# First tokens with tokens on partitions in a fused attention and feed-forward kernel; the low bits of the weights move from GpSimd to ScalarE

## The chip, the cores and the metric

The kernel runs on one core of a Trainium2 chip. The metric is device time in microseconds (us), from the launch of the program to its end; the time before is 574.05 us (median of 3 runs, 573.91 to 575.09). Engines are named as in the profile: PE is TensorE, DVE VectorE, ACT ScalarE, POOL GpSimd, SP SyncE, whose queue issues the DMAs.

## The reference

```
q, k, v: (4, 8, 576, 64)   M_prev: (4, 8, 64, 64)   z_prev: (4, 8, 64)   beta: (8,)
a     = softmax(q @ k.T / 8, causal);        local = a @ v
q_p   = elu(q) + 1
mem   = (q_p @ M_prev) / (q_p @ z_prev + 1e-6)
g     = sigmoid(beta)
attn  = g * mem + (1 - g) * local            # (4, 8, 576, 64)
x     = attn as 2304 tokens x 512 (head and feature together)
out   = relu(x @ w_in) ** 2 @ w_out          # w_in 512 x 2048, w_out 2048 x 512
```

Inputs and output are float32.

## The kernel before

**Products.** The feed-forward part runs in fp16 with each operand as a high and a low half: three matmuls stand for one product (hi·hi, hi·lo, lo·hi; L940 to L942 for `up`, the first layer, and L912 to L914 for `oacc`, the second).

**Weights.** They come as 32 pieces of 512 KB: eight groups of four, w_in and w_out in turn. The float32 bits of a piece arrive in a 64-bit number. `to_float` puts them together: ACT shifts the upper word (L194), the low three bits are made by POOL for two pieces of three (L191, 21 pieces) and by DVE for the third (L193, 11 pieces), and DVE joins both into `fc` (L196). `weight_scale` finds one scale for a group: 16 matmuls (`gr`, L222), a maximum over rows (L225), one over partitions (L203, L204), a power of two (L210, L213) and its reciprocal. `halves` then writes the high half (ACT, L240) and the low half (DVE, L241). The first 16 pieces use one set of buffers, the others a second one: loads from piece 16 on (L266, SP's queue) wait until buffers of the first set are free, and the float piece 28 takes the buffer of piece 20, so it waits for the halves of 20.

**Attention.** A unit is one batch, one pair of heads and some tiles of tokens; batches 0 and 1 run their tiles 1 and 2 for all four head pairs, then 3 and 4, batches 2 and 3 all four tiles at once. Scores are `sp` (L558), their maxima `mx` (L579), exponentials `e` (L599), the normed weights `a` (L637, L639), which go through a DMA transpose to `aT`; `acc` (L663) is weights times values, added into `feat` (L666). The memory part is `pe` (elu, L463 to L475), `pm` (L522) and `nm` (L527, L531).

**First tokens.** Tile 0 of every batch, 64 tokens x 4 batches, is computed on its own in `first_tokens`, in two groups g of two batches, so that the feed-forward part has a first block of 256 tokens (`moe(0)`) before any attention unit is done. Both heads of a pair stand on the partitions, a feature on each, tokens beside one another. For one group: scores, `phi` (elu features, then the norm `nr`, its reciprocal, 16 matmuls `rb` that spread it over partitions, and a product), `softmax`, and `outputs`: transposed weights `px`, the sum `xp` of memory and local part (features on partitions), its squares, their sums over features for each token by matmuls with ones (`nm`), a power of two and its reciprocal over 128 x 128 (`qn`, `sn`, L390), the product `xs` (L392), high half (L394) and low half (L395), which go straight into `xT`, the operand of `moe(0)`.

**Later blocks.** `moe(1)` to `moe(6)` take 256 tokens each from `feat`: squares (L689), scale, halves `hl` (L696, L697), a DMA transpose into `xT` (L698). The last two blocks are computed together in another way.

**Order.** `ORD` merges generators: the first attention unit with 17 steps of weights, then units 1 to 3 with the weights' steps up to 34 and `moe(0)`, then the other units one after the other. From these a tile scheduler writes each engine's order; each engine works through its list in that order. Up to unit 3 a unit's rows follow one another, from unit 4 (`FIRST`) on the next unit is begun ("whole": loads, scores and features ahead) before the rows of this one. Values of `gate` ("v", "s", "t") mark instructions of the first tokens behind which other work of the same engine is held.

Of the kernel before, what the change touches and what calls it, by code (L numbers as in the profile page):

```python
# [78 lines left out]
FIRST = 4  # L79
WE = 8  # L80
# [17 lines left out]
def fused_kernel(ctx: ExitStack, tc: tile.TileContext, t0_d, kk_d, qv_d, beta, w_in, w_out, out):  # L98
# [22 lines left out]
    onesb = cp.tile([P, P], BF16, name="onesb")  # L121
    nc.vector.memset(onesb, 1.0)
# [36 lines left out]

    gate = {}  # L160
# [143 lines left out]
    def first_tokens(tp, ahead):  # L304
# [4 lines left out]
        tr, sp, et, ft = ({} for _ in range(4))  # L309
# [27 lines left out]
        def phi(g):  # L337
            q, z = part(g, 0), tr[g][:, 2 * GD : TA]
            ft[g] = f = tp.tile([P, GN, D], F32, tag="f", name="f", bufs=2)
            t2 = tp.tile([P, GN], F32, tag="t2", name="t2", bufs=2)  # L340
# [4 lines left out]
            for i, hd in pairs():  # L345
                nc.tensor.matmul(nr[hd, i : i + 1], f[hd, i], z[hd, i : i + 1], start=True, stop=True)
            nc.vector.scalar_tensor_tensor(out=t2, in0=nr, scalar=1e-6, in1=gib, op0=ALU.add, op1=ALU.mult)
            nc.vector.reciprocal(t2, t2)
            rb = ps.tile([P, GN, D], F32, tag="av", name="rb", bufs=2)
            for i, hd in pairs():  # L350
                nc.tensor.matmul(
                    rb[hd, i], t2[hd, i : i + 1].to_broadcast([D, D]), ident[hd, hd], start=True, stop=True
                )
            nc.vector.tensor_tensor(out=f, in0=f, in1=rb, op=ALU.mult)

        def softmax(g):
# [10 lines left out]
            nc.vector.reciprocal(t1, t1)  # L367
            gate["v"] = nc.vector.tensor_tensor(out=e, in0=e, in1=t1[:, :, None].to_broadcast(bc), op=ALU.mult)

        def outputs(g):  # L370
# [5 lines left out]
            m, v = part(g, TA), part(g, TA + GD)  # L376
            xp = ps.tile([P, GN, D], F32, tag="av", name="xp", bufs=2)
            for i, hd in pairs():
                at_i = xp[hd, i % NP * GB + i // NP]
                nc.tensor.matmul(at_i, m[hd, i], ft[g][hd, i], start=True, stop=False)  # L380
                gate["t"] = nc.tensor.matmul(at_i, v[hd, i], ex[hd, i], start=False, stop=True)
            xb = xp.rearrange("p (i b) q -> p i (b q)", b=GB)
            sq = tp.tile([P, NK, P], BF16, tag="sq", name="sq", bufs=2)
            nc.scalar.activation(sq, xb, AF.Square)
            nm = ps.tile([P, P], F32, tag="acc", name="nm0", bufs=2)
            for k in range(NK):
                nc.tensor.matmul(nm, onesb, sq[:, k], start=k == 0, stop=k == NK - 1)
            q, s = (tp.tile([P, P], F32, tag=t, name=t, bufs=1) for t in ("qn", "sn"))
# [4 lines left out]
            hi, lo = (xT[:, g, k * NK : (k + 1) * NK] for k in range(2))
            gate["s2"] = nc.scalar.copy(hi, xs)  # L394
            gate["v2"] = nc.vector.tensor_tensor(out=lo, in0=xs, in1=hi, op=ALU.subtract)  # L395
            qc = ps.tile([P, 1], F32, tag="acc", name="qc", bufs=2)
            nc.tensor.matmul(qc, q.bitcast(BF16).rearrange("p (n t) -> p n t", t=2)[:, :, 1], identb[:, :1], start=True, stop=True)
            nc.scalar.activation(tok0[:, g : g + 1], qc, AF.Square, scale=WSC / HSC)
# [707 lines left out]
```

## Time and profile before

| | |
|---|---|
| time, median of 3 runs | 574.05 us (573.91 to 575.09) |
| the profiled execution: its own time | 575.25 us |
| its span, first to last instruction | 573.5 us |
| PE busy | 531.8 us (93%), clock 0.973 |
| DVE busy | 456.3 us (80%) |
| ACT busy | 398.1 us (69%) |
| POOL busy | 60.1 us (10%) |

Busy time is that of instructions that compute; PE's clock is the share of full speed that was granted. A row of the timeline gives start, duration, engine, line, output and inputs; what stands in brackets at its end is the engine's idle time before it and what ended it. Starts of neighbouring instructions are a little nearer than durations say, since they overlap at the ends. The profiled execution's 575.25 us is 1.75 us more than its span and 1.20 us above the median.

### The profile page before, as it was taken

How to read it: one execution, taken by the hardware profiler on the slowest of the kernel's cores; microseconds unless marked ns; L12 is line 12 of the kernel's file. 1: busy time of each engine (PE TensorE's matmuls, PEld its weight loads, DVE VectorE, ACT ScalarE, POOL GpSimd, SP SyncE). 2: the span in 40 equal slices, each digit the busy share in tenths (PEclk: the TensorE clock that was granted, in tenths of full speed). 3: DMA queues.
4: the chain of work that ended last, by engine and by line, in shares of the span. 5: the costliest groups of instructions: out<-in, count | busy, mean ns of one | idle time of the engine just before them, and what ended most of it. 6: DMA issues, size and time to landing. Idle time of an engine off the chain costs nothing.

```text
span 573.5 us, 12883 instructions
## 1 busy us (share of the span) xinstructions
PE 531.8 (93%) x4903; PEld 378.3 (66%) x4903; DVE 456.3 (80%) x1413; ACT 398.1 (69%) x853; POOL 60.1 (10%) x41
## 2 busy tenths in 40 slices
PE   6587997799989799999999999999899999999997
PEld 6375774576757577667767667767666756447766
DVE  6989789998888978999779878887685888544745
ACT  3566897776787797988868887887676644457352
POOL 3660584001010000000000000000000000000000
PEclk9957999699999999999999999999999999999999
DMA  8921796365657876987396476562656510100002
GB/s 311 405 98 38 259 353 167 82 141 122 136 138 150 150 164 147 164 175 197 95 151 121 119 153 114 81 117 69 112 105 74 98 20 2 38 0 1 2 1 73
DMA packets 131022, 70.87 MB, mean 124 GB/s; under 512 B 113296, under 2 KB 119440, under 8 KB 130960
## 3 DMA queue, kind: packets, MB, share of 16 engines
q1 hardware_dynamic: 130960, 70.05, 51.8%
q8 instruction: 38, 0.62, 0.4%
q14 instruction: 24, 0.20, 0.1%
HBM read 37.53 MB, written 4.72 MB: 74 GB/s over the span
## 4 chain that ended last, share of the span: by engine, by line
PE 32%; DVE 29%; ACT 12%; DMA 7%; issue 4%; SPq 0%; ACTq 0%; DVEq 0%
DVE a L639 6%; DVE e L579 6%; DMA aT<-a 4%; ACT e L599 4%; PE seven L815 4%; PE up L940 3%; PE up L941 3%; PE up L942 3%; PE oacc L913 3%; PE oacc L912 3%; PE oacc L914 3%; ACT a L637 3%; PE seven L788 2%; PE seven L786 2%; PE seven L787 2%
## 5 line engine op out<-in xcount | busy, mean ns | idle before, releaser
L940 PE MATMUL up<-xT,w 128*128 128x256 f16 x448 | 123.7, 277 | 3.2 <-DMA xT<-hl 2.6
L941 PE MATMUL up<-xT,w 128*128 128x256 f16 x448 | 123.7, 276 | 0.0
L942 PE MATMUL up<-xT,w 128*128 128x256 f16 x448 | 123.6, 276 | 0.0
L599 ACT ACTIVATE e<-e,mx 128x320 f32<-128x320 f32 (+3 forms) x128 | 77.5, 607 | 45.2 <-DVE feat L666 27.5
L912 PE MATMUL oacc<-w,gh 128*128 128x512 f16 x224 | 85.0, 379 | 2.3 <-ACT gh L949 2.3
L913 PE MATMUL oacc<-w,gh 128*128 128x512 f16 x224 | 84.9, 379 | 0.0
L914 PE MATMUL oacc<-w,gl 128*128 128x512 f16 x224 | 81.2, 379 | 0.8 <-DVE gl L952 0.6
L639 DVE SCALAR_TENSOR_TENSOR a<-e,a 128x128 f16<-128x128 f32 x116 | 65.7, 575 | 20.3 <-ACT a L637 19.9
L637 ACT ACTIVATE a<-e 128x128 f16<-128x128 f32 x116 | 54.8, 522 | 4.8 <-DMA aT<-a 4.5
L941 PEld LDWEIGHTS <-w 128*128 128x128 f16 x448 | 44.5, 99 | 14.2 <-issue 3.2
L940 PEld LDWEIGHTS <-w 128*128 128x128 f16 x448 | 44.3, 99 | 11.3 <-DMA xT<-hl 0.5
L942 PEld LDWEIGHTS <-w 128*128 128x128 f16 x448 | 44.4, 99 | 7.3
L663 PE MATMUL acc<-vs,aT 128*128 128x64 f16 x1138 | 41.8, 193 | 7.8 <-DMA aT<-a 5.4
L663 PEld LDWEIGHTS <-aT 128*128 128x128 f16 x1138 | 38.6, 98 | 15.4 <-DMA aT<-a 7.7
L579 DVE CUSTOM_DVE_ANT_0 e<-sp,mask 128x320 f32<-128x320 f32 (+3 forms) x128 | 46.9, 416 | 0.9 <-PE pxa L614 0.9
L191 POOL TENSOR_SCALAR raw<-raw 128x512 uint32<-128x512 uint16 x21 | 45.0, 2141 | 19.8 <-DMA raw<-in_w_in_dram 10.4
L952 DVE TENSOR_TENSOR gl<-r,gh 128x512 f16<-128x512 f32 x56 | 38.7, 693 | 6.1 <-ACT gh L949 5.5
L946 ACT ACTIVATE r<-up,gam 128x512 f32<-128x512 f32 x48 | 32.2, 673 | 14.8 <-PE up L942 12.3
L914 PEld LDWEIGHTS <-gl 128*128 128x128 f16 x224 | 21.5, 98 | 23.0 <-DVE gl L952 2.0
L815 PEld LDWEIGHTS <-g 128*128 128x128 f16 x336 | 32.7, 98 | 5.4 <-DVE g L741 1.2
L912 PEld LDWEIGHTS <-gh 128*128 128x128 f16 x224 | 21.9, 98 | 21.4 <-ACT gh L949 3.1
L947 ACT ACTIVATE r<-r 128x512 f32<-128x512 f32 x56 | 34.8, 624 | 0.7
(196 smaller groups left out, 1076.5 us busy)
## 6 DMA issues: line engine op xcount, KB each, us to landing
raw<-in_w_in_dram SPq DMA_DIRECT2D x16, 512.0 KB, 6.5
raw<-in_w_out_dram SPq DMA_DIRECT2D x16, 512.0 KB, 7.6
vv<-in_qv_dram SPq DMA_DIRECT2D x16, 320.0 KB, 3.2
kd<-in_kk_dram SPq DMA_DIRECT2D x16, 288.0 KB, 3.4
out_dram<-o SPq DMA_DIRECT2D x12, 256.0 KB, 2.6
qm<-in_qv_dram SPq DMA_DIRECT2D x8, 321.0 KB, 3.4
qm<-in_qv_dram SPq DMA_DIRECT2D x8, 193.0 KB, 3.4
vv<-in_qv_dram SPq DMA_DIRECT2D x8, 192.0 KB, 4.9
```

The costliest lines, as they stand in the source:

```text
L579: nc.vector.tensor_tensor_reduce(out=e[:, h, ka:kb], in0=sps[:, h, cs], in1=mask[:, 448 - q0 + ka : 448 - q0 + kb], scale=-0.125, scalar=3 ...
L599: ex = nc.scalar.activation(e[:n, h, :ke], e[:n, h, :ke], AF.Exp, bias=bs, scale=-1.0, accum_out=sm[:n, h : h + 1])
L637: nc.scalar.mul(av[:, :, o0 : o0 + w], x, SC)
L639: nc.vector.scalar_tensor_tensor(out=av[:, :, o0 + w : o0 + 2 * w], in0=x, scalar=SC, in1=av[:, :, o0 : o0 + w], op0=ALU.mult, op1=ALU.sub ...
L663: nc.tensor.matmul(acc[:n, h], lhs[:, :n], rhs, start=x == 0, stop=x == len(mms) - 1)
L815: mms.append(nc.tensor.matmul(x[:, blk], g[j][:, i0, a, blk, p], t_side(j, p, m, i1), start=j == js[0] and p == n == 0, stop=j == js[-1] a ...
L912: nc.tensor.matmul(acc[t], gh[:, u, ts], w_out_op(f, 0), start=f == f0, stop=False)
L913: nc.tensor.matmul(acc[t], gh[:, u, ts], w_out_op(f, 1), start=False, stop=False)
L914: nc.tensor.matmul(acc[t], gl[:, u, ts], w_out_op(f, 0), start=False, stop=f == f1)
L940: nc.tensor.matmul(up[:, u, :], w_in_op(f, k, 0), xT[:, :, k], start=k == 0, stop=False)
L941: nc.tensor.matmul(up[:, u, :], w_in_op(f, k, 0), xT[:, :, NK + k], start=False, stop=False)
L942: nc.tensor.matmul(up[:, u, :], w_in_op(f, k, 1), xT[:, :, k], start=False, stop=k == NK - 1)
```

## The change

**First tokens.** From the features on, tokens stand on partitions. z becomes a 65th column of M, so the 16 matmuls that make M's part (`pm0`) also give the norm, in two halves of four pairs each; `nr` and `rb` are gone, and so are the matmuls that join memory and local part. The softmax's weights are not normed before the product with the values; `pv0` is scaled as it is read, and the memory part is added to it. Squares are summed on ACT (one instruction for each of the two batches, with the sum beside), a single matmul with `both` adds the two heads' halves, and the power of two and the reciprocal are 128 x 2. High and low halves go into a tile `hl`, and one DMA transpose for each group (L413, SP's queue) brings them into `xT`. `moe(0)` reads `xT` through another view (`x_op`); w_in's rows are permuted by the host, and `feat` has its columns in the same new order.

**Low bits.** The 21 pieces of POOL go to ACT (L198: Identity with a scale of 2^-13 and a bias tile `under`); POOL makes none. The 11 pieces of DVE stay.

**Units.** `WA = 0` makes units 1 to 3 begin one ahead too, within each call of `attn`.

```diff
 def to_float(n):
-        if n % 3 > 0:
-            top = rw.bitcast(U16).rearrange("p n (t h) -> p n t h", h=2)[:, :, 0, 1]
-            nc.gpsimd.tensor_scalar(out=u0, in0=top, scalar1=2.0**-13, scalar2=7.0, op0=ALU.mult, op1=ALU.min)
+        top = rw.bitcast(U16).rearrange("p n (t h) -> p n t h", h=2)[:, :, 0, 1]
+        if n % 3 > 0:
+            put(n, "s", nc.scalar.activation(u0, top, AF.Identity, scale=2.0**-13, bias=under))
 def phi(g):
-            nr = ps.tile([P, GN], F32, tag="acc", name="nr", bufs=2)
...
-            nc.vector.tensor_tensor(out=f, in0=f, in1=rb, op=ALU.mult)
 def softmax(g):
-            nc.vector.reciprocal(t1, t1)
-            gate["v"] = nc.vector.tensor_tensor(out=e, in0=e, in1=t1[:, :, None].to_broadcast(bc), op=ALU.mult)
+            gate["v"] = nc.vector.reciprocal(t1, t1)
+        def memory(g):
+            for i0 in range(0, GN, NP):
+                pm = ps.tile([P, NP, ZW], F32, tag="av", name="pm0", bufs=2)
+                for i, hd in pairs()[2 * i0 : 2 * (i0 + NP)]:
+                    nc.tensor.matmul(pm[hd, i - i0], f[hd, i], mz[hd, i], start=True, stop=True)
...
+            nc.vector.reciprocal(t2, t2)
+            for n, pm in pms:
+                nc.vector.tensor_tensor(
+                    out=f[:, n], in0=pm[:, :, :D], in1=t2[:, n, None].to_broadcast([P, NP, D]), op=ALU.mult
+                )
 def outputs(g):
-                nc.tensor.matmul(at_i, m[hd, i], ft[g][hd, i], start=True, stop=False)
-                gate["t"] = nc.tensor.matmul(at_i, v[hd, i], ex[hd, i], start=False, stop=True)
+                gate["t"] = nc.tensor.matmul(pv[hd, i], ex[hd, i], v[hd, i], start=True, stop=True)
+            nc.vector.tensor_tensor(out=y, in0=pv, in1=st[g][:, :, None].to_broadcast(bc), op=ALU.mult)
+            nc.vector.tensor_tensor(out=x, in0=x, in1=y, op=ALU.add)
...
+            for b in range(GB):
+                nc.scalar.activation(hl[:, 0, b], xb[:, b], AF.Square, accum_out=ss[:, b : b + 1])
...
+                gate["s2"] = nc.scalar.activation(hi, xb[:, b], AF.Copy, scale=s1)
+                gate["v2"] = nc.vector.scalar_tensor_tensor(
+                    out=lo, in0=xb[:, b], scalar=s1, in1=hi, op0=ALU.mult, op1=ALU.subtract
+                )
+            nc.sync.dma_start_transpose(out=xT[:, g], in_=hl.rearrange("p x b n -> p (x b n)"))
 def attn(i0, i1):
-            if i >= FIRST:
-                for x in (rows,) if i == FIRST else ():
+            if i >= WA:
+                for x in (rows,) if i == i0 else ():
```

On SP the two transposes stand behind the loads of the first 16 pieces: the first ahead of the loads `kd`, `qm`, `kd` of units 2 and 3, the second behind them and ahead of the loads of piece 16 and later. Three places in the orders of DVE and ACT follow; names with a number are single buffers, `w_...` the halves of one weight piece.

DVE in the kernel before, from the second group's `xs` (first tokens) to its low half `xT`, with low halves of pieces 9 to 11 between them:

```order
L392 TENSOR_TENSOR xs<-xp,sn 128x512
L204 TENSOR_REDUCE kap<-gr 128x1
L241 SCALAR_TENSOR_TENSOR w_669<-fc,win_s,w_669 128x512
L241 SCALAR_TENSOR_TENSOR w_672<-fc,win_s,w_672 128x512
L210 TENSOR_SCALAR kap<-kap 128x1
L241 SCALAR_TENSOR_TENSOR w_675<-fc,win_s,w_675 128x512
L579 ISA e,mx<-sp,mask 128x320
L579 ISA mx 128x1
L579 ISA e,mx<-sp,mask 128x320
L579 ISA mx 128x1
L921 TENSOR_SCALAR kj<-tok_80,kap 128x2
L395 TENSOR_TENSOR xT<-xs,xT 128x512
```

The same place after the change, from the second group's last low half `hl` to the low half of piece 8, `w_609`:

```order
L410 SCALAR_TENSOR_TENSOR hl<-f,sn,hl 128x256
L211 TENSOR_REDUCE kap<-gr 128x1
L220 TENSOR_SCALAR win_e<-win_e 128x1
L217 TENSOR_SCALAR kap<-kap 128x1
L241 RECIPROCAL win_s<-win_e 128x1
L220 TENSOR_SCALAR kap<-kap 128x1
L236 TENSOR_TENSOR wout_s<-kap 128x1
L237 RECIPROCAL wout_s<-wout_s 128x1
L238 TENSOR_TENSOR kap<-kap,win_e 128x1
L946 TENSOR_SCALAR kj<-tok_80,kap 128x2
L248 SCALAR_TENSOR_TENSOR w_609<-fc,win_s,w_609 128x512
```

The four low halves of pieces 8 to 11, which stood ahead of the first tokens' last instruction, now stand behind it.

ACT in the kernel before, from the high halves of piece 7 through the second group's `wx` to its high half `xT` and squares `sq` of `xp`:

```order
L240 ACTIVATE w_622<-fc,wout_s 128x512
L398 ACTIVATE tok_80<-qc 128x1
L375 COPY wx<-px_348 128x512
L463 ACTIVATE pe<-qm 128x256
L194 ACTIVATE raw<-raw 128x512 x8
L394 CAST xT<-xs 128x512
L384 ACTIVATE sq<-xp 128x512
```

The same stretch after the change, from behind the second group's `wx` to its squares (L400):

```order
L482 ACTIVATE pe<-qm 128x256
L198 ACTIVATE raw<-raw,under 128x512
L201 ACTIVATE raw<-raw 128x512 x2
L198 ACTIVATE raw<-raw,under 128x512
L201 ACTIVATE raw<-raw 128x512
L198 ACTIVATE raw<-raw,under 128x512
L201 ACTIVATE raw<-raw 128x512 x2
L198 ACTIVATE raw<-raw,under 128x512
L201 ACTIVATE raw<-raw 128x512
L198 ACTIVATE raw<-raw,under 128x512
L201 ACTIVATE raw<-raw 128x512 x2
L400 ACTIVATE hl,s_344<-f 128x256 x2
```

Where eight instructions on raw words stood there are now thirteen, five of them for low bits (L198), and the high half of the first group (L409) has moved ahead of them and of the high halves of pieces 4 to 7.

DVE in the kernel before, at the float piece 28 (`fc`, L196 behind the third of the four low halves of pieces 20 to 23, `w_1288` to `w_1297`):

```order
L485 TENSOR_REDUCE vx<-vv 128x1
L921 TENSOR_SCALAR kj<-tok_80,kap 128x2
L666 SCALAR_TENSOR_TENSOR feat<-acc,sm,feat 128x64 x4
L487 TENSOR_SCALAR vx<-vx 128x1
L241 SCALAR_TENSOR_TENSOR w_1288<-fc,wout_s,w_1288 128x512
L241 SCALAR_TENSOR_TENSOR w_1291<-fc,wout_s,w_1291 128x512
L241 SCALAR_TENSOR_TENSOR w_1294<-fc,wout_s,w_1294 128x512
L196 SCALAR_TENSOR_TENSOR fc<-raw 128x512
L241 SCALAR_TENSOR_TENSOR w_1297<-fc,wout_s,w_1297 128x512
```

The same place after the change (`w_1231` to `w_1240` are the halves of pieces 20 to 23, `w_1288` and `w_1291` those of 24 and 25):

```order
L598 ISA e,mx<-sp,mask 128x192
L598 ISA mx 128x1
L248 SCALAR_TENSOR_TENSOR w_1231<-fc,wout_s,w_1231 128x512
L248 SCALAR_TENSOR_TENSOR w_1234<-fc,wout_s,w_1234 128x512
L248 SCALAR_TENSOR_TENSOR w_1237<-fc,wout_s,w_1237 128x512
L248 SCALAR_TENSOR_TENSOR w_1240<-fc,wout_s,w_1240 128x512
L203 SCALAR_TENSOR_TENSOR fc<-raw 128x512
L248 SCALAR_TENSOR_TENSOR w_1288<-fc,win_s,w_1288 128x512
L203 SCALAR_TENSOR_TENSOR fc<-raw 128x512
L248 SCALAR_TENSOR_TENSOR w_1291<-fc,win_s,w_1291 128x512
```

The halves of pieces 20 to 23 no longer stand behind rows of later attention units (the sums over `vv` of a further unit, `feat` of four tiles); what stood there before has moved behind them.

## Rows read from the trace of the kernel before

**Rows 1.** The page: busy time of each engine, share of the span, instructions.

```profile
PE 531.8 (93%) x4903; PEld 378.3 (66%) x4903; DVE 456.3 (80%) x1413; ACT 398.1 (69%) x853; POOL 60.1 (10%) x41
```

**Rows 2.** Windows: stretch, length, busy time by engine, PE clock, DMA share, GB/s.

```profile
0.00:40.15 40.15, 26.21 (x409) 23.47 (x410) 31.43 (x79) 18.83 (x32) 23.39 (x19) 0.84 0.76 291
40.15:54.60 14.45, 11.19 (x92) 8.28 (x93) 14.41 (x48) 10.45 (x29) 0.84 (x1) 0.85 0.14 38
54.60:91.93 37.33, 37.33 (x285) 28.80 (x284) 30.73 (x90) 31.92 (x85) 23.94 (x12) 0.95 0.71 262
91.93:108.08 16.15, 10.02 (x69) 5.52 (x66) 15.93 (x62) 11.32 (x24) 4.32 (x3) 0.83 0.65 149
160.00:573.50 413.50, 395.52 (x3618) 276.28 (x3616) 318.06 (x994) 288.67 (x611) 3.35 (x3) 1.00 0.49 97
```

**Rows 3.** Timeline of DVE, first tokens' end and weights to piece 28.

```profile
53.99 0.68 DVE L395 TENSOR_TENSOR xT<-xs,xT 128x512 f16<-128x512 f32 x1
...
58.75 2.74 DVE L241 SCALAR_TENSOR_TENSOR w<-fc,wout_s,w 128x512 f16<-128x512 f32 x4 [0.25 <-ACT w L240]
...
91.26 0.67 DVE L196 SCALAR_TENSOR_TENSOR fc<-raw 128x512 uint32<-128x512 uint32 x1
...
105.42 2.07 DVE L241 SCALAR_TENSOR_TENSOR w<-fc,wout_s,w 128x512 f16<-128x512 f32 x3
107.40 0.68 DVE L196 SCALAR_TENSOR_TENSOR fc<-raw 128x512 uint32<-128x512 uint32 x1
```

**Rows 4.** Timeline of PE, first up matmuls and the wait for piece 28.

```profile
54.17 0.61 PE L940 MATMUL up<-xT,w 128*128 128x256 f16 x2
...
108.14 0.61 PE L222 MATMUL gr<-fc 128*128 128x128 bf16 x4 [1.41 <-DVE fc L196]
```

**Rows 5.** Groups on DVE by form, 0 to 54 us: busy, mean ns.

```profile
L241 DVE SCALAR_TENSOR_TENSOR w<-fc,win_s,w 128x512 f16<-128x512 f32 x8 | 6.1, 789 | 0.0
...
L390 DVE RECIPROCAL sn<-qn 128x128 f32<-128x128 f32 x2 | 1.9, 942 | 0.0
...
L368 DVE TENSOR_TENSOR w<-w,t 128x512 f32<-128x512 f32 x2 | 1.6, 781 | 0.0
...
L392 DVE TENSOR_TENSOR xs<-xp,sn 128x512 f32<-128x512 f32 x2 | 1.4, 676 | 0.0
L354 DVE TENSOR_TENSOR f<-f,rb 128x512 f32<-128x512 f32 x2 | 1.3, 670 | 0.0
...
L533 DVE TENSOR_TENSOR feat<-pm,nm 128x256 f32<-128x256 f32 x1 | 0.4, 414 | 0.0
```

**Rows 6.** One line's instructions, low bits on POOL: ns min/median/max.

```profile
L191 POOL TENSOR_SCALAR raw<-raw x21: 1975/2053/2514, 9.6 to 93.2; 128x512 uint32<-128x512 uint16 x21
```

**Rows 7.** One line's instructions, the join on DVE.

```profile
L196 DVE SCALAR_TENSOR_TENSOR fc<-raw x32: 674/682/1153, 9.1 to 112.1; 128x512 uint32<-128x512 uint32 x32
```

**Rows 8.** Groups on ACT by form, 0 to 115 us.

```profile
L194 ACT ACTIVATE raw<-raw 128x512 f32<-128x512 f32 x32 | 20.7, 677 | 10.1 <-DMA raw<-in_w_in_dram 6.9 <-DMA raw<-in_w_out_dram 3.1
...
L463 ACT ACTIVATE pe<-qm 128x256 f32<-128x256 f32 x6 | 2.5, 411 | 0.0
```

**Rows 9.** Timeline of ACT, the weights' upper words of pieces 8 to 15, and squares.

```profile
36.66 0.58 ACT L375 COPY wx<-px 128x512 f32<-128x512 f32 x1
37.15 0.42 ACT L463 ACTIVATE pe<-qm 128x256 f32<-128x256 f32 x1
37.46 4.62 ACT L194 ACTIVATE raw<-raw 128x512 f32<-128x512 f32 x8
```

**Rows 10.** SP's queue: waits to 115 us: in total, times, longest.

```profile
SPq L419 <- PE sp L558: 21.1, 3, 17.0
...
SPq L266 <- DVE w L241: 14.0, 4, 11.3
```

**Rows 11.** Timeline of SP, loads around the second set of buffers.

```profile
47.85 0.33 SPq L419 DMA_DIRECT2D kd<-in_kk_dram  x1
59.53 2.79 SPq L266 DMA_DIRECT2D raw<-in_w_in_dram  x4
```

**Rows 12.** One line's instructions, transposes into xT: issue in ns, landing in us.

```profile
L698 SPq DMA_TRANSPOSE xT<-hl x12: 1232/1283/2306, 119.9 to 378.9; - x12
...
DMA to landing us min/median/max: 3.2/4.0/5.6
```

**Rows 13.** Who PE waited for, 115 to 573.5 us.

```profile
PE up L940 <- DMA xT<-hl: 2.6, 1, 2.6
```

More of the change, by code (lines that the diff above doesn't have):

```diff
@@ L120, in fused_kernel @@
     tok0 = cp.tile([P, 2], F32, name="tok0")
-    onesb = cp.tile([P, P], BF16, name="onesb")
-    nc.vector.memset(onesb, 1.0)
+    both = cp.tile([P, 2, D], BF16, name="both")
+    for h in range(2):
+        nc.vector.tensor_tensor(out=both[:, h], in0=identb[:, :D], in1=identb[:, D:], op=ALU.add)
     mask = cp.tile([P, MW], BF16, name="mask")
@@ L158, in fused_kernel @@
     nc.vector.tensor_copy(mask0[D:], mask[D:, 512 : 512 + D])
+    under = cp.tile([P, 1], F32, name="under")
+    nc.vector.memset(under, 2.0**-14 - 0.5)
     gate = {}
@@ L308, in first_tokens @@
         bc = [P, GN, D]
-        tr, sp, et, ft = ({} for _ in range(4))
+        tr, sp, et, ft, st = ({} for _ in range(5))
         for g in range(ng):
@@ L337, in phi @@
         def phi(g):
[L338 removed]
+            q = part(g, 0)
             ft[g] = f = tp.tile([P, GN, D], F32, tag="f", name="f", bufs=2)
[L340 removed]
             nc.scalar.activation(f, q, AF.Exp)
@@ L375, in outputs @@
             gate["s"] = nc.scalar.copy(ex, px)
[L376 to L377 removed]
+            v, x, y = part(g, TV), ft[g], et[g]
+            pv = ps.tile([P, GN, D], F32, tag="acc", name="pv0", bufs=2)
             for i, hd in pairs():
[L379 to L381 removed]
@@ L382, in outputs @@
[L382 to L388, printed above, removed]
+                gate["t"] = nc.tensor.matmul(pv[hd, i], ex[hd, i], v[hd, i], start=True, stop=True)
@@ L389, in outputs @@
+            nm = ps.tile([P, GB], F32, tag="acc", name="nm0", bufs=2)
+            nc.tensor.matmul(
+                nm, both.rearrange("p h x -> p (h x)"), ss.bitcast(BF16).rearrange("p (n t) -> p n t", t=2)[:, :, 1], start=True, stop=True
+            )
             root(q, 0x7F000000, 1, 2.0**64 * XSC, nm)
             nc.vector.reciprocal(s, q)
-            xs = tp.tile([P, NK, P], F32, tag="wx", name="xs", bufs=2)
-            nc.vector.tensor_tensor(out=xs, in0=xb, in1=s[:, None, :].to_broadcast([P, NK, P]), op=ALU.mult)
@@ L393, in outputs @@
[L393 to L398, printed above, removed]
+            for b in range(GB):
+                hi, lo, s1 = hl[:, 0, b], hl[:, 1, b], s[:, b : b + 1]
+                gate["s2"] = nc.scalar.activation(hi, xb[:, b], AF.Copy, scale=s1)
+                gate["v2"] = nc.vector.scalar_tensor_tensor(
+                    out=lo, in0=xb[:, b], scalar=s1, in1=hi, op0=ALU.mult, op1=ALU.subtract
+                )
@@ L400, in first_tokens @@
+            nc.sync.dma_start_transpose(out=xT[:, g], in_=hl.rearrange("p x b n -> p (x b n)"))
+            for b in range(GB):
+                hd = slice(b * D, (b + 1) * D)
+                nc.scalar.activation(tok0[hd, g : g + 1], q[hd, b : b + 1], AF.Square, scale=WSC / HSC)
         sp0 = ps.tile([P, ng, GN, D], F32, tag="s", name="sp0")
@@ L898, in moe, with x_op @@
         xT, osc = xq[n]
+        x0 = xT.rearrange("p g (x b m) (h q) -> p g x b m h q", x=2, b=GB, h=2)
         pend = []
+        def x_op(k, part):
+            return x0[:, :, part, :, k // 2, k % 2] if lead else xT[:, :, part * NK + k]
         acc = []
@@ L1020, in unit @@
         early = i < NEF and max(order[i][2]) < 4
-        return attention(*order[i], ld, after, i < NEARLY, i < NES, early, ap, i >= FIRST)
+        return attention(*order[i], ld, after, i < NEARLY, i < NES, early, ap, i >= WA)
     def attn(i0, i1):
@@ L1084 @@
     bt = _np.concatenate([_np.repeat(bt.reshape(NP, 2).T, D, axis=0), _np.tile(bt, (P, 1))], axis=1)
+    wi = _np.asarray(inputs["moe_w_in"]).reshape(2, 2, 2, D, FF).transpose(0, 2, 1, 3, 4)
+    wi = _np.ascontiguousarray(wi.reshape(DM, FF))
     host = {
@@ L1089 @@
         "beta": _np.ascontiguousarray(bt),
-        "w_in": _np.ascontiguousarray(inputs["moe_w_in"]).view(_np.int64),
+        "w_in": wi.view(_np.int64),
         "w_out": _np.ascontiguousarray(inputs["moe_w_out"]).view(_np.int64),
```

46 lines of the change are left out of this document (26 added, 20 removed).

## The prediction

> **What bounds the kernel now.** I read the page first, then a table of stretches, then the timelines of the stretches in which PE is not full. PE is busy for 531.8 of 573.5 us [rows 1], so 41.7 us of idle PE are all that an edit off PE's work can win, and the table says where they lie [rows 2]: 13.9 us before 40.15, 3.3 up to 54.60, none up to 91.93, 6.1 up to 108.08, and 18.0 in the long part from 160 on, where PE is 96% full at full clock. The change acts on the first four stretches. In the first two DVE is the engine that sets the pace at the end: from 40.15 to 54.60 it is busy for 14.41 of 14.45 us, and the last row of that queue, the second group's low half of the first tokens at 53.99, releases the first `up` matmul at 54.17 [rows 3, 4]. From there PE is full until 91.93, with ACT at 31.92 of 37.33 us, 5.4 idle, and DVE at 30.73. Then DVE is the bound again: 15.93 of 16.15 us, while PE waits for the float piece 28, which waits for the third of the four low halves of pieces 20 to 23 at 105.42 to 107.40; the 16 matmuls of its scale stand ahead of ready `up` matmuls in PE's list, and PE's last wait there (1.41 us) ends on that piece at 108.14.
>
> **The first tokens, work.** For one group DVE loses the product with `rb` (670 ns), the norming of the weights (781), the reciprocal of 128 x 128 (942), the one product `xs` (676) [rows 5] and half of two powers-of-two steps. It gains two products of 128 x 256 read from PSUM (414 each, by the nearest row, L533, of that size and kind [rows 5]), a scaled read of `pv0` (676, by L392), a sum of two SBUF tiles (some 680, by the same form), a second small step for the norm and two short reciprocals (some 0.15 each). The sum is about -3.3 and +2.6, so -0.6 us for a group, -1.3 for both. ACT gets two squares and two high halves of 128 x 256 in place of one each of 128 x 512: 411 ns each [rows 8] for four, against two of some 600, and sums to read beside: +0.5 to +1.0 us for a group.
>
> **The low bits.** POOL's 21 instructions of 2053 ns [rows 6] end. ACT gets 21 of the length of its upper words, 677 ns, or 4.62 / 8 = 0.58 from start to start [rows 8, 9]: 12.2 to 14.2 us in all, 10 of them with pieces 1 to 14, 10 in the stretch 54.60 to 91.93, one behind. I take 0.6 each; the form with a bias tile and 16-bit input is not in the trace, so from 0.41 (half the columns, L463 [rows 8]) to 0.77 (L194's 677 ns with nothing overlapped and a tenth of a us on top). What DVE wins is that its own work isn't stretched beside POOL: the join is 682 ns at the median and 1153 at the longest [rows 7]; the 8 low halves of the first part average 789 against 2.07 / 3 = 690 later [rows 3, 5]. Over all rows of DVE to 108 us I sum 4 to 5 us of such stretch; that is gone.
>
> The Trainium skill ("SBUF — State Buffer", section "Who interferes with whom") has a stronger rule: a DVE instruction with two inputs from SBUF contends with GpSimd's reads for one shared port pair, held for a whole instruction. If a join waited for half a POOL instruction on the average, 21 of them would give 21 us; the longest join [rows 7] lies only 0.47 us above the median, so the trace does not bear that out as a whole.
>
> **First `up`.** Two chains lead to it. DVE: in the changed order the low halves of pieces 8 to 11 (4 x 0.69 = 2.7 us), one pair of maxima and both long reciprocals no longer stand ahead of the second group's low half; with 1.3 us less work and the stretch gone the low half comes 7 to 8 us earlier, at 46 to 47. ACT: the second group's copy `wx` (36.66 before, [rows 9]) comes 4 to 5 us earlier, since the scale of group 1 no longer waits for joins behind POOL; behind it stand 13 raw instructions, 13 x 0.58 = 7.5 in place of 4.62, then squares, four exponentials and the high halves: about 45.5. Both give a low half at 46.3. But the way into `xT` now is a DMA transpose: 1.28 us to issue and 4.0 to land [rows 12]: 51.6 in place of 54.17, so -2.6 us. Ends: with 3.2 to land and 44.5 for the low half 49.0 (-5.2); with 2.31 and 5.6 us and the low half at 46.3 it is 54.2 (0). The second transpose stands on SP behind `kd`, `qm`, `kd` of units 2 and 3, which wait for scores of earlier units (up to 17.0 us [rows 10]); the last of them went at 47.85 [rows 11], and comes 1 to 2 us earlier with units begun ahead, so I count no wait for it; the rival below prices it.
>
> **From there to piece 28.** Loads of piece 16 and later wait for the second set of buffers, that is for the halves of pieces 12 and on (58.75, loads at 59.53 [rows 3, 11]); these now stand some 4 us earlier in DVE's list. In the stretch that follows ACT gets 10 x 0.6 = 6.0 us, which the idle 5.4 us nearly take [rows 2], so ACT becomes as full as PE there: the float piece 27 (91.26 [rows 3]) comes with the start, less about 0.5 us. Behind it DVE has, before piece 28, 15.9 us of work in the trace; in the changed order the halves of pieces 20 to 23 stand ahead of rows of a further attention unit, and of the rows that remain I sum 11.2 us: up to 4.7 us less. But PE is not paid for all of it: rows that are put off come right behind, and PE waits for those (`sp` for maxima, `acc` for `vs`) as it did before; of the 6.1 us of idle PE I take 1 us as won, with 0 and 4.2 as ends.
>
> **Later.** One wait of 2.6 us, `up` of the second block for its transposed input [rows 13], hangs on the order of `hl` against the sixth `gl`; in the changed order `hl` stands earlier there. Half of it, 1.3 us, is my value, 0 and 2.6 the ends. Units 1 to 3 begun ahead move scores and maxima forward; the DVE and ACT rows are the same in number, PE's work is unchanged, and I count nothing. The host's permutation of w_in and of `feat`'s columns costs nothing: products of 128 x 64 are as long in any column order, and the write of `feat` strides over 64 columns (414 ns before in the same count of elements [rows 5]). Fewer fp32 matmuls of the first tokens (two groups) lie before 54 us, where PE is not the bound.
>
> **Sum.** -2.6 (start) + 0.5 (ACT) - 1.0 (piece 28) - 1.3 (later) = -4.4, rounded to -4.5, from 575.25 for the profiled execution: 570.75. That execution is 1.20 above the median, so 569.5 us beside 574.05.
>
> **Rivals.**
> 1. ACT becomes the engine that sets the pace from the first tokens to piece 28. For it: ACT works in order, and the low bits stand in lumps ahead of `r`, `gh` and the high halves on which PE and the next scales hang; 5.4 us of idle time in the 37.33 is all there is. It decides from the point where ten low bits cost more than 0.54 us each. At 0.77, 10 of them overrun the idle time by 2.3 us; the lump of 13 ahead of the second group's squares, at 0.77 for its five, is 1.0 longer; the extra 0.5 to 1.0 us of the two groups comes on top, 1.5 in all; and a late `gh` leaves PE idle or at half clock (0.83 to 0.85 of full clock in the two stretches with gaps [rows 2]) for some 2 us more. The first tokens' gain of 2.6 is eaten: 575.25 - 2.6 + 2.3 + 1.0 + 1.5 + 2.0 = 579.5, and with half of the later wait won 578.2, so 577 beside the median. Against: before 54.6 ACT has long waits for loads, 10.1 us on upper words alone [rows 8].
> 2. The way through SP takes the whole gain at the start. For it: 2.31 + 5.6 us at the longest [rows 12], behind loads that wait for units 0 and 1. The first `up` then stays at 54 to 55, DVE's and ACT's lead is lost there, and of the rest only 0.5 to 1.5 us come through: 573.3 us.
> 3. DVE gains more than the stretches that I can see, because the releases that POOL gave late also held DVE's and PE's scale chains: in the first 40 us PE idles for 13.9 us and POOL is busy for 23.4 [rows 2]. The start at 49.0 (-5.2), 4.2 at piece 28, 2.6 later: -12.0, 562 us. The shared port of the Trainium skill's page named above would be one way to it.
>
> **How the numbers follow.** Forecast 0.50, rival 1 0.22, rival 2 0.15, rival 3 0.13. What a measurement of this kernel can tell from no change is about 0.2%, 1.15 us. Faster: 0.47 of the forecast, 0.13, and 0.06 of rival 2: 0.66. Same: 0.03, 0.05 of rival 2, 0.01 of rival 1: 0.09; slower: 0.21 and 0.04: 0.25. The forecast alone spans 566 to 572.5; the range reaches to rival 3 at 562 and past rival 1 at 577, to 578.
>
> **What would show it.** In the profile after: POOL's busy time at some 15 us; DVE's join without lengths near 1150; L198 on ACT at 0.6 us; the second transpose issued at 46 to 47 and the first `up` at 49 to 54; loads of piece 16 three to five us before 59.5; piece 28's join near 100 instead of 107.4; no wait of `up` for `xT` near 190. The forecast is wrong if ACT has under 2% idle time between the first `up` and piece 28 and PE waits for `gh` or for high halves there; if the first `up` comes after 54; or if PE's idle time from 160 us on, 18.0 before, grows by more than 3 us because units or blocks fall otherwise against each other.

## The result and the profile after

The changed kernel takes 582.57 us (median of 4 runs, 580.75 to 584.56) where the kernel before takes 574.38: the ratio is 1.014, interval [1.0105, 1.0179]. It is slower, and the prediction of 569.5 us was wrong in size and in sign. The profiled execution has a span of 582.8 us; its own time, 584.56 us, is the longest of the four.

The page's busy times, against [rows 1]:

```profile
PE 527.8 (91%) x4767; PEld 370.4 (64%) x4767; DVE 452.9 (78%) x1421; ACT 413.1 (71%) x884; POOL 14.9 (3%) x20
```

PE has 4.0 us less to do, DVE 3.4, ACT 15 more. PE's idle time is 55.0 us where it was 41.7. The table of stretches, against [rows 2] (length, busy time of PE, PEld, DVE, ACT, POOL, PE clock, DMA share, GB/s):

```profile
0.00:40.15 40.15, 22.01 (x323) 18.25 (x323) 33.22 (x94) 27.01 (x50) 2.94 (x9) 0.74 0.86 306
40.15:54.60 14.45, 10.96 (x71) 8.70 (x72) 12.07 (x50) 13.21 (x40) 2.12 (x2) 0.76 0.20 32
54.60:91.93 37.33, 34.82 (x246) 24.46 (x244) 28.71 (x96) 34.46 (x77) 0.85 (x1) 0.91 0.77 269
91.93:108.08 16.15, 13.36 (x97) 10.01 (x97) 13.64 (x40) 10.35 (x28) 0.84 (x1) 0.89 0.24 50
108.08:160.00 51.92, 45.51 (x404) 30.77 (x403) 49.12 (x161) 41.56 (x92) 5.94 (x5) 0.97 0.71 149
160.00:582.80 422.80, 401.18 (x3635) 278.19 (x3632) 316.12 (x986) 286.47 (x601) 2.21 (x2) 0.99 0.47 95
```

The stretch behind 108.08 in the kernel before, which [rows 2] left out:

```profile
108.08:160.00 51.92, 51.50 (x440) 35.97 (x440) 45.71 (x147) 36.86 (x79) 4.22 (x3) 0.95 0.57 122
```

Up to 40.15 us PE has 4.2 us less to do and idles for as much longer; the first `up` comes earlier all the same. What is new are idle 2.5 us at 54.60 to 91.93, 6.4 at 108.08 to 160 (0.4 before) and 21.6 from 160 on (18.0). At piece 28 there is the gain that was looked for: 2.8 idle in place of 6.1.

The steps that the prediction worked out one by one, in the timelines of DVE, SP and PE, against [rows 3, 4, 11]:

```profile
46.47 0.47 DVE L410 SCALAR_TENSOR_TENSOR hl<-f,sn,hl 128x256 f16<-128x256 f32 x1
...
54.05 2.73 DVE L248 SCALAR_TENSOR_TENSOR w<-fc,wout_s,w 128x512 f16<-128x512 f32 x4
...
96.28 0.68 DVE L203 SCALAR_TENSOR_TENSOR fc<-raw 128x512 uint32<-128x512 uint32 x1
```

```profile
46.97 2.14 SPq L413 DMA_TRANSPOSE xT<-hl  x1
54.82 2.83 SPq L273 DMA_DIRECT2D raw<-in_w_in_dram  x4
```

```profile
50.98 0.42 PE L966 MATMUL up<-xT,w 128*128 128x256 f16 x1
...
97.01 0.54 PE L229 MATMUL gr<-fc 128*128 128x128 bf16 x4 [2.06 <-DVE fc L203]
```

The last low half of the first tokens starts at 46.47 (46.3 forecast), the first `up` at 50.98 (51.6), the loads of piece 16 come 4.7 us earlier, piece 28 at 96.28 in place of 107.40. And yet the time went up. The instructions of the low bits and of the join, against [rows 7] (count, ns min/median/max):

```profile
L203 DVE SCALAR_TENSOR_TENSOR fc<-raw x32: 678/684/733, 9.0 to 100.1; 128x512 uint32<-128x512 uint32 x32
```

```profile
L198 ACT ACTIVATE raw<-raw,under x21: 747/768/816, 9.6 to 87.2; 128x512 uint32<-128x512 uint16 x21
```

The join's long cases are gone; the low bits cost 768 ns on ACT, the upper end of the range, not 0.6.

How far each kernel is, by `up` matmuls of L940 (L966) that had run at a time (of 448; a matmul at a border counts twice, some records are missing):

| by us | 60 | 80 | 100 | 120 | 160 | 200 | 240 | 320 |
|---|---|---|---|---|---|---|---|---|
| before | 9 | 25 | 32 | 50 | 97 | 134 | 181 | 257 |
| after | 19 | 32 | 37 | 61 | 94 | 137 | 173 | 254 |

At 200 us the two are level in these, in `oacc` (61 and 63) and in `acc` (329 and 331). At 240 the changed kernel is 8 `up`, 3 `oacc` and 12 `acc` behind: the early lead is used up by 160 to 200 us, and the loss begins behind 200 us, in a part of the program that the change does not touch. Between 200 and 240 us PE idles for 0.4 us before and for 6.2 after (columns as above):

```profile
200.00:240.00 40.00, 39.57 (x382) 28.50 (x380) 34.48 (x132) 33.69 (x79) 0.00 (x0) 1.00 0.80 158
```

```profile
200.00:240.00 40.00, 33.77 (x319) 23.41 (x318) 29.38 (x109) 28.93 (x69) 0.00 (x0) 1.00 0.61 126
```

What PE waits for there, 200 to 250 us, before and after (total, times, longest):

```profile
PE vt L489 <- DVE feat L533: 0.7, 2, 0.4
```

```profile
PE oacc L937 <- ACT gh L975: 3.8, 4, 2.0
PE acc L682 <- DVE feat L552: 1.8, 1, 1.8
PE vt L508 <- DVE feat L552: 0.6, 1, 0.6
```

ACT is late with `gh`, and the timeline says why: it stands still for q's load. The rows of ACT, then those of SP and of PE, at the longest of these waits:

```profile
228.25 0.67 ACT L972 ACTIVATE r<-up,gam 128x512 f32<-128x512 f32 x1
230.77 0.42 ACT L482 ACTIVATE pe<-qm 128x256 f32<-128x256 f32 x1 [1.85 <-DMA qm<-in_qv_dram]
231.09 1.03 ACT L656 ACTIVATE a<-e 128x128 f16<-128x128 f32 x2
232.02 0.61 ACT L973 ACTIVATE r<-r 128x512 f32<-128x512 f32 x1
232.54 0.66 ACT L471 CAST kh<-kd 128x576 fp32r<-128x576 f32 x1
233.10 0.61 ACT L975 CAST gh<-r 128x512 f16<-128x512 f32 x1
```

```profile
223.83 2.71 SPq L662 DMA_TRANSPOSE aT<-a  x1
226.63 1.04 SPq L442 DMA_DIRECT2D qm<-in_qv_dram  x2
```

```profile
233.77 0.39 PE L937 MATMUL oacc<-w,gh 128*128 128x512 f16 x1 [2.02 <-ACT gh L975]
```

The load of `qm` stands on SP behind a transpose that waits for `a`; ACT begins with it at 230.77, after 1.85 us of waiting, and the square and `gh` of the feed-forward part, whose input had been ready since 228.9, stand behind. PE's `oacc` starts at 233.77, after 2.02 us of waiting for `gh`. Of the four waits for `gh`, this one and one of 0.66 us stand right behind such a stop of ACT; the other two (0.83 and 0.28 us) do not.

### The profile page after: what moved, and what is told of

It is laid out like the page before. It is cut to its first block, busy times and chain, and to the rows that moved or that the text cites. A ratio compares the mean times of both kernels' runs of the same rounds, so it can differ in the third digit from the quotient of the medians.

```text
span 582.8 us, 12609 instructions
## 1 busy us (share of the span) xinstructions
PE 527.8 (91%) x4767; PEld 370.4 (64%) x4767; DVE 452.9 (78%) x1421; ACT 413.1 (71%) x884; POOL 14.9 (3%) x20
## 4 chain that ended last, share of the span: by engine, by line
PE 34%; DVE 31%; ACT 15%; DMA 13%; issue 5%; SPq 1%; POOL 0%; ACTq 0%; DVEq 0%
DVE e L598 5%; DVE a L658 5%; PE seven L834 4%; ACT e L618 4%; DMA aT<-a 3%; DMA qm<-in_qv_dram 3%; PE oacc L939 3%; PE oacc L937 3%; PE oacc L938 3%; PE up L967 3%; PE up L966 3%; PE up L968 3%; PE acc L682 3%; DMA raw<-in_w_in_dram 3%; PE seven L807 2%
## 5 line engine op out<-in xcount | busy, mean ns | idle before, releaser
L966 PE MATMUL up<-xT,w 128*128 128x256 f16 x448 | 123.3, 275 | 0.1
L937 PE MATMUL oacc<-w,gh 128*128 128x512 f16 x224 | 86.5, 386 | 6.3 <-ACT gh L975 6.1
L938 PE MATMUL oacc<-w,gh 128*128 128x512 f16 x224 | 86.0, 384 | 0.0
L658 DVE SCALAR_TENSOR_TENSOR a<-e,a 128x128 f16<-128x128 f32 x116 | 64.5, 566 | 18.6 <-ACT a L656 18.2
L966 PEld LDWEIGHTS <-w 128*128 128x128 f16 x448 | 44.5, 99 | 10.8
L972 ACT ACTIVATE r<-up,gam 128x512 f32<-128x512 f32 x48 | 32.4, 674 | 15.5 <-PE up L968 12.8
L939 PEld LDWEIGHTS <-gl 128*128 128x128 f16 x224 | 21.6, 98 | 25.0 <-issue 2.7
L685 DVE SCALAR_TENSOR_TENSOR feat<-acc,sm,feat 128x64 f32<-128x64 f32 x128 | 29.1, 276 | 9.1 <-PE acc L682 9.0
```

The source lines that it names most:

```text
L658: nc.vector.scalar_tensor_tensor(out=av[:, :, o0 + w : o0 + 2 * w], in0=x, scalar=SC, in1=av[:, :, o0 : o0 + w], op0=ALU.mult, op1=ALU.sub ...
L937: nc.tensor.matmul(acc[t], gh[:, u, ts], w_out_op(f, 0), start=f == f0, stop=False)
L938: nc.tensor.matmul(acc[t], gh[:, u, ts], w_out_op(f, 1), start=False, stop=False)
L939: nc.tensor.matmul(acc[t], gl[:, u, ts], w_out_op(f, 0), start=False, stop=f == f1)
L966: nc.tensor.matmul(uo, w_in_op(f, k, 0), x_op(k, 0), start=k == 0, stop=False)
```

## The experiments

Theory A: what costs is another order of the later units, which any edit of the first 100 us brings about, since the scheduler lays all of it out anew. Theory B: the low bits on ACT. Theory C: the first tokens' new form. Theory D, in the later runs, is B and C together: the new work, in whatever order. Ratios are to the kernel before, run on the same chip; "PE's last n" are instructions that stand at PE's end in the same sequence as before (of 7974 in the new form). In the changed kernel the old sequence comes back late: for the last 53 of DVE's 1421 rows, from 500.6 us on.

**The parts apart.**

```diff
 e1_units:   -WA = 0
             +WA = 4
 e2_pool:    -put(n, "s", nc.scalar.activation(u0, top, AF.Identity, ...))      # the changed kernel
             +nc.gpsimd.tensor_scalar(out=u0, in0=top, scalar1=2.0**-13, scalar2=7.0, ...)
 e3_act:     the kernel before, with the opposite of e2's edit
 e5_tokens:  both edits, e1's and e2's: the first tokens' new form alone
```

> The changed kernel with units 1 to 3 begun as before (WA = 4); first tokens and low bits on ACT stay. Theory A (the new order of units and loads is what costs: PE's idle time from 200 us on, 18 us after the change against 10 before, goes away when the units stand as before): 572 to 577 us, and ACT's waits for qm loads between 100 and 480 us fall from 12.6 us to under 4. Theory B (low bits on ACT are the price, by my rival 1): 581 to 584, as changed. Theory C (the first tokens' new form costs, by its transposes and by PE at half clock before 54 us): 581 to 584.

> The changed kernel with the 21 low bits back on POOL. Theory A: 580 to 585, since the units stand as in the changed kernel. Theory B: 572 to 576, ACT's busy time back to some 399 us. Theory C: 581 to 585.

> The kernel before with the low bits on ACT and nothing else changed. Theory A: 572 to 576, no change beyond 2 us. Theory B: 581 to 584, with PE waiting for gh or for the halves between 54 and 108 us. Theory C: 572 to 576.

> The kernel before with the first tokens' new form alone (low bits on POOL, units 1 to 3 as before). Theory A: 569 to 575. Theory B: 569 to 573. Theory C: 581 to 585, with the loss before 100 us.

| | us | ratio, interval |
|---|---|---|
| e1_units | 580.25 | 1.008 [1.004, 1.012] |
| e2_pool | 591.05 | 1.028 [1.022, 1.034] |
| e3_act | 579.90 | 1.009 [1.006, 1.012] |
| e5_tokens | 586.62 | 1.018 [1.011, 1.026] |

No theory fits. Every part is slower alone, and they do not add: low bits on ACT cost 4.7 us in the kernel before and save 8.5 in the changed one (591.05 to 582.57). e5, whose profiled execution (582.29 us) is its fastest, has a lead at 80 us (33 `up` and 52 `acc` against 25 and 41) and loses it, as the changed kernel does, later: at 200 us 133 and 328 against 134 and 329, at 320 us 260 and 666 against 257 and 743. That fits the order, which is another one in e2, e3 and e5.

**The same work in another order.**

```diff
-    merge((attn(1, FIRST), 52), (wsteps(34), 16), (first(), 18))
+    merge((attn(1, FIRST), 50), (wsteps(34), 16), (first(), 18))   # n1_b50: before; n2_b54: 54
                                                     # v1_after54: the changed kernel with 54; v2_tokens54: e5 with 54
 x3_ahead: the kernel before with the change's WA = 0 and its two places in unit and attn
```

> The kernel before with one merge weight of ORD at 50 in place of 52: the same instructions in another order from PE's row 604 on. Theory A (the order from 90 us on that the scheduler makes is what costs, whatever caused another order): slower than before by 3 to 15 us, 578 to 590, with more idle PE time from 160 us on (18 before). Theory D (the new work itself costs: transposes, low bits on ACT, other first tokens): within 2 us of before.

> The kernel before with the same weight at 54: another order from PE's row 296 on. Theory A: 578 to 590. Theory D: within 2 us of before.

> The changed kernel with the weight at 54: the same instructions in another order. Theory A: away from the changed kernel's 582.6 by 3 us or more, to either side (572 to 592). Theory D: 581 to 585.

> The first tokens' new form alone (586.6 us in its first order) with the weight at 54. Theory A: away from 586.6 by 3 us or more; with the early lead of 4 us that the first form showed kept and an order as good as before's, 570. Theory D: 584 to 589.

> The kernel before with units 1 to 3 begun ahead and nothing else. Theory A: another order from PE's row 292 on, so 578 to 590. Theory D: within 2 us of before.

| | us | ratio, interval |
|---|---|---|
| n1_b50 | 584.50 | 1.018 [1.014, 1.022] |
| n2_b54 | 582.89 | 1.013 [1.009, 1.018] |
| v1_after54 | 580.97 | 1.013 [1.008, 1.018] |
| v2_tokens54 | 584.17 | 1.016 [1.012, 1.020] |
| x3_ahead | 582.72 | 1.014 [1.011, 1.017] |

Theory A holds where it counts: the kernel before, with a number of its merge changed and not one instruction, is 9 to 11 us slower (584.50 and 582.89 against 573.96 on that chip), as slow as the changed kernel. n1 has PE's first 604 instructions in the old order, and 133 `up` and 329 `acc` at 200 us (134 and 329 before); at 320 us it is 76 `acc` behind (667 against 743) and 3 `up` ahead (260 against 257). With the same instructions its PE idles for 46.7 us (41.7 before) and is busy for 535.6 (531.8): its granted clock is 0.96, 0.94 and 0.97 at 200 to 240, 240 to 270 and 400 to 450 us, where it was 1.00. The other half, that the changed kernel moves by 3 us or more with another order, was a miss (1.6 and 2.4 us): other orders differ little from one another; it is the order of the kernel before that stands apart.

**The new work in the old later order.** A merge weight of 40 gives e5's work PE's last 5794 instructions as before; e1 has 5908 of them; with half of ACT's low bits it is 6748. By DVE's rows the old order begins at 205 us in x1, 198 in e1, 149 in x2 and 114 in y1. x2 leaves out half of the low bits on ACT: the join takes those of the first 256 columns for the other half too.

```diff
 x1_tokens40: e5 with
-    merge((attn(1, FIRST), 52), ...
+    merge((attn(1, FIRST), 40), ...
 x2_half_act: e1 with w = 256 for ACT's pieces
-            put(n, "s", nc.scalar.activation(u0, top, ...))
+            put(n, "s", nc.scalar.activation(u0[:, :w], top[:, :w], ...))
 y1_five_act: e1 with
-        if n % 3 > 0:
+        if n % 3 > 0 and not (n < 16 and n % 3 == 1):   # POOL makes these, ACT the five others
```

> The first tokens' new form alone, with the merge weight at 40: the last 5794 of PE's 7974 instructions stand as in the kernel before (in the form that took 586.6 us only the last 741 did). Theory A (the later order is the price): 568 to 574, PE's idle time from 160 us on back at 18, and the early lead of some 4 us at 80 us kept or lost at piece 28. Theory D (the new work is the price, in any order): 582 to 588.

> The changed kernel with units 1 to 3 as before and ACT's low bits made for the first 256 columns of a piece only (the join takes these for the other half as well, so the lowest three bits of half of the weights are those of other weights). PE's last 6748 instructions stand as in the kernel before, as the last 5908 did with whole low bits (580.25 us). Theory A with ACT as the pace setter from 57 to 108 us (the lead is eaten there, with 5 us lost at ACT's 100% in 70 to 90): 570 to 575, ACT under 95% busy in 70 to 90 us. If ACT's pace is not what costs the 5 us: 578 to 582.

> The first tokens' new form, units 1 to 3 as before, and low bits on ACT for pieces 1, 4, 7, 10 and 13 alone (16 pieces stay on POOL); merge weight 52. PE's last 7250 of 7974 instructions stand as in the kernel before. Theory A with ACT as pace setter where it makes all low bits: 569 to 573, faster than before, since ACT has 3 us more to do in place of 13, all before 54 us. Theory D: 580 to 586.

| | us | ratio, interval |
|---|---|---|
| x1_tokens40 | 574.33 | 0.997 [0.994, 0.999] |
| x2_half_act | 571.34 | 0.995 [0.993, 0.997] |
| y1_five_act | 574.03 | 0.998 [0.995, 1.001] |

So the first tokens' new form is not slow: in the old later order it takes 12 us less than in the one that the scheduler made for it, and 2 us less than the kernel before. This settles A against C. x1 and y1 came out a little above what theory A had expected (568 to 574 and 569 to 573), and y1 is level with the kernel before. e1, with the old order from 198 us on, is 1.3% above x2, the two intervals far apart: all of ACT's low bits cost 6 us there against POOL's (x1) and 9 against half of ACT's (x2), both run on another chip than e1. The place in x2's expectation was wrong, though: ACT is full from 70 to 90 us in both (third number from the left after the length is DVE, the fourth ACT):

```profile
70.00:90.00 20.00, 17.88 (x140) 12.30 (x138) 16.22 (x51) 20.00 (x46) 1.03 (x1) 1.00 0.75 259
90.00:110.00 20.00, 14.36 (x86) 9.28 (x84) 18.09 (x55) 14.46 (x35) 0.84 (x1) 0.83 0.22 48
110.00:135.00 25.00, 22.48 (x165) 13.68 (x164) 22.69 (x72) 18.25 (x39) 2.26 (x2) 1.00 0.64 135
```

```profile
70.00:90.00 20.00, 16.70 (x119) 12.51 (x119) 16.35 (x46) 20.00 (x49) 0.84 (x1) 0.87 0.86 302
90.00:110.00 20.00, 14.40 (x68) 8.08 (x67) 15.41 (x58) 10.85 (x28) 2.24 (x2) 0.67 0.35 84
110.00:135.00 25.00, 24.18 (x205) 17.92 (x203) 24.87 (x86) 22.77 (x47) 3.10 (x2) 0.96 0.58 125
```

The first block is e1, the second x2. Up to 110 us x2 idles no less; it idles 0.8 us in place of 2.5 from 110 to 135. x2's profiled execution (576.89 us) is the slowest of its 12, 5.6 above the median, so these windows show 3.3 of the 9 us at most. The two also differ in the order of some 840 early PE instructions, so the share of ACT's pace in the 1.3% is not clean.

**Late loads of q.** ACT's waits for loads of q between 160 and 450 us (total, times, longest), in the kernel before and in the changed one:

```profile
ACT qh L446 <- DMA qm<-in_qv_dram: 1.8, 2, 1.5
...
ACT pe L463 <- DMA qm<-in_qv_dram: 0.3, 1, 0.3
```

```profile
ACT qh L465 <- DMA qm<-in_qv_dram: 7.4, 4, 2.9
...
ACT pe L482 <- DMA qm<-in_qv_dram: 3.2, 2, 1.9
```

Summed, 2.1 and 10.6 us. All the kernels with another later order have 8.5 to 12.4 (e2, e3, e5, n1, n2, v1, v2, x3), those with the old one 1.0 to 6.6 (x1, y1, x2, e1, from the least). The wait alone does not make the loss, though: PE's idle time between 160 and 450 us is 13.1 us in the kernel before and 16.2 in the changed one, but 9.7 in e3, 12.0 in v1 and 12.8 in v2, where ACT waits for q for 8.5, 12.0 and 10.1 us. To see what it does in the changed kernel, these loads were taken off SP's queue, where they stand behind transposes that wait for DVE (units 8 and later):

```diff
-            nc.sync.dma_start(qm[:, c0:c1], qv_d[b, p, :, c0:c1])
+            (nc.gpsimd if i >= AHEAD else nc.sync).dma_start(qm[:, c0:c1], qv_d[b, p, :, c0:c1])
 z1_after_qm_pool: the changed kernel; z2_n1_qm_pool: n1_b50; z3_before_qm_pool: before; w2_five_qm_pool: y1
 z4_after_qm_act, w1_tokens_qm_act: nc.scalar in place of nc.gpsimd, in the changed kernel and in e5
```

> The changed kernel with the loads of q (qm) of units 8 and later issued by POOL's queue in place of SP's, where they stand behind transposes of a that wait for DVE. Theory Q (in an order that was not chosen these loads land late, ACT stands for them, 10.6 us between 160 and 450 us against 2.1 in the kernel before, and gh behind them is late for PE): ACT's waits for qm fall under 4 us and the time to 573 to 579. Theory R (these waits only follow, the loss has its place elsewhere): ACT waits for something else as long, 580 to 585.

> The kernel before with the merge weight at 50 (584.5 us) and the same loads on POOL's queue. Theory Q: 574 to 580, ACT's waits for qm from 10.4 us to under 4. Theory R: 582 to 587.

> The kernel before with the same loads on POOL's queue. PE's last 5387 instructions keep their order. Theory Q: 572 to 576, since ACT waits for qm for 2.1 us only. Theory R: 572 to 578.

> The changed kernel with these loads issued by ACT's queue, each in ACT's own order; PE's last 3397 instructions stand as in the kernel before. Theory Q: ACT's waits for qm under 4 us, 574 to 581. Theory R: 580 to 585.

> The first tokens' new form alone in the order that took 586.6 us, with the loads of q of units 8 and later on ACT's queue. Theory Q (late loads of q are what a new order costs): 574 to 579, ACT's waits for qm from 12.4 us to under 3. Theory R: 582 to 588.

> The first tokens' new form with five pieces' low bits on ACT (574.0 us) and the same loads on POOL's queue; PE's last 5387 instructions stand as in the kernel before. Theory Q: 570 to 574, little to win since ACT waits 3.7 us there. Theory R: 573 to 577.

| | us without, with | ACT's wait for qm, us | ratio with, interval |
|---|---|---|---|
| z1, changed kernel, POOL | 582.57, 576.07 | 10.6, 3.3 | 1.000 [0.998, 1.002] |
| z4, changed kernel, ACT | 582.57, 575.74 | 10.6, 1.9 | 1.000 [0.997, 1.003] |
| w1, first tokens alone, ACT | 586.62, 578.76 | 12.4, 6.9 | 1.007 [1.004, 1.010] |
| z2, before in another order, POOL | 584.50, 580.95 | 10.4, 5.2 | 1.009 [1.006, 1.011] |
| z3, before, POOL | 574.38, 575.49 | 2.1, 3.2 | 1.000 [0.998, 1.002] |
| w2, five pieces on ACT, POOL | 574.03, 575.83 | 3.7, 4.7 | 1.001 [0.998, 1.004] |

1.6 of w1's 6.9 us stand ahead of `o`, which does not read q. What theory Q forecast for the changed kernel came true: it comes back to the time of the kernel before with this edit, by either queue, and the edit does nothing in the fast order. Between 200 and 240 us, where PE idled for 6.2 us, it idles for 0.4 in z1 (shown first) and 1.4 in z4, and no wait for `gh` is left there:

```profile
200.00:240.00 40.00, 39.62 (x367) 28.08 (x366) 30.99 (x116) 28.38 (x67) 3.26 (x7) 1.00 0.58 130
```

```profile
200.00:240.00 40.00, 38.57 (x396) 28.21 (x394) 35.99 (x139) 34.60 (x81) 0.00 (x0) 1.00 0.72 163
```

From 160 to 450 us PE's idle time falls from 16.2 to 11.5 and 13.8 us, 4.7 and 2.4 of the 7.5 and 9.3 us that the profiled spans differ by; the rest lies elsewhere. The wait of `oacc` for `gh` over that whole stretch is 3.9 us in z1, 5.3 in the changed kernel:

```profile
PE oacc L937 <- ACT gh L975: 3.9, 3, 1.6
```

Where the wait only halves (z2, w1), a good part of the loss is left: 0.9 of 1.8% in z2, 0.7 of 1.8% in w1. w1 fits theory Q: PE's idle time between 160 and 450 us falls from 18.8 to 12.5 us. z2 does not show it: there it is 15.0 us, 15.7 without the edit, and 2.4 of the 3.4 us between the two spans are idle time before 108 us, where both kernels have the same order. Several forecasts missed: z2's time (574 to 580) and wait (under 4), w1's wait (under 3) and w2's time (570 to 574). In the fast orders the wait was short, and the edit leaves it so (z3, w2).

One reservation weighs: a moved load also changes the order, and not a little. DVE's rows in z1 are the changed kernel's for the first 329 of 1421 only, to 126 us, and z4 has the old order again for the last 395, from 347 us on. So z1 and z4 are other orders as well as other queues, and their return to 576 us is not shown to be the queue's work alone. What speaks against chance is that none of the eight other kernels with a new later order came under 579.9 us, that both edits take away the stop at 200 to 240 us, and that w1, which keeps e5's rows on DVE to 179 us, gains as well.

## Why the prediction was wrong

**The step that failed** is in "Later": "Units 1 to 3 begun ahead move scores and maxima forward; the DVE and ACT rows are the same in number, PE's work is unchanged, and I count nothing." The instructions are the same in number, but not their order, and the order is worth 8 to 11 us by itself (n1, n2, x3). x3 is this part alone: 1.014. In its place the runs showed a stop of PE: 6.2 us idle between 200 and 240 us where it was 0.4; 3.8 of it are waits for `gh`, 2.7 of these right behind a late load of q. The prediction compared the orders at three places of the first 110 us and took the 413.5 us behind 160 as they were, against what the order of SP would have shown: apart from the two new transposes, the loads `kd`, `qm`, `vv` stand in other places from the 39th row of the kernel before on. Of its own signs of failure the last one came true: PE's idle time from 160 us on grew by 3.6 us, and by 6 us from 108 to 160.

**The start** was right to 0.6 us, in part by luck. The low half (46.47), the freed loads and the join without its long cases came as forecast. But the times to landing of [rows 12] are counted from the start of the issue, so 1.28 + 4.0 counts the issue twice, and the 0.5 us of the low half itself was left out: the transpose is issued at 46.97, lands 3.5 us later, and the first `up` starts at 50.98 right behind PE's work on `pxa`. Rival 2, a late `xT`, is out.

**Piece 28** came 11.1 us earlier, and PE's idle time there fell by 3.3 us where 1 was counted. It was not kept: the waits moved to 108 to 160 us, where PE waits 3.8 us for maxima (`sp` behind `mx`), one of the waits that the prediction had named; before the change it waited for none there.

**The low bits on ACT** were mis-sized: 768 ns in place of 0.6 us, 21 x 0.17 = 3.5 us more than counted, at the price that rival 1 had. ACT was 92% busy from 54.60 to 91.93 (34.46 of 37.33), full from 70 to 90, and PE waited for it (`gr` behind `r`, 1.8 us, [rows 2] had none). Rival 1 named the right engine and nearly the size for e1; it came out at 577 us as a sum, but the changed kernel's own loss seems to lie elsewhere: z1 and z4 keep every low bit on ACT and are level with the kernel before.

**The later wait** of `up` for its transposed input [rows 13] is gone, as half counted; others took its place.

**Rival 3** fell: POOL's stop took the long joins away, and the 12 us did not come. By the Trainium skill's rule on the shared port ("SBUF — State Buffer", "Who interferes with whom") the joins had something to win; in these traces it is 1.2 us in all: four of the 32 joins took 789 to 1153 ns, the others 694 at most, and after the change the longest takes 733.

In sum, by the runs: the first tokens in the old later order -0.3% (x1), with all low bits on ACT +0.8% (e1), with units begun ahead and so another order +1.4% (the changed kernel). The steps don't add up to causes, though, since with the loads of q off SP's queue, and another order with it, the whole 1.4% is gone (z1, z4), low bits on ACT included. Left open is how much of e1's 0.8% is ACT's pace and how much its own waits for q (6.6 us), and what the kernels lose whose PE idles no longer behind 160 us than before (e3, v1, v2).

## What to carry to other kernels

A kernel whose order was found by trying numbers has a time that belongs to that order: before a small gain from an edit is forecast, compare the whole order before and after, the DMA queue's above all, and take another order with the same instructions as the measure of what chance does (here 8 to 11 us, about twice the gain that was forecast). A load that stands in a queue behind transposes that wait for a computed value is late as soon as that value is; an engine that reads it in order then holds back work that had nothing to wait for. Putting loads of inputs on a queue of their own, or ahead of such waits, is worth trying: it came with a gain of 6.5 to 7.9 us in two kernels here, of 3.5 in a third and of nothing in the two fast ones.

## What the runs showed of the hardware

Identity on ACT, 16-bit input, 32-bit output and a bias tile, takes 771 ns on the average for 128 x 512 (747 to 816), 95 more than Prelu without a bias on 32-bit words (676). A load of q takes 0.54 us of POOL to issue at the median (z1) and 0.42 of SP (the changed kernel). PE's granted clock in the first 40.15 us was 0.74 on the average in place of 0.84, with PE busy for 22.0 in place of 26.2 us there.
